# Nine tokens of a head on each partition, and 32x32 turns on VectorE in place of DMA and TensorE ones

## The chip, the cores and the metric

The kernel runs on one core of a Trainium2 chip. The metric is the device time of one execution in microseconds (us); smaller is better. The five engines of the core are TensorE (PE, with its weight loads PEld), VectorE (DVE), ScalarE (ACT), GpSimd (POOL) and SyncE (SP, which here only issues DMAs). Each engine works through its own list of instructions in order.

## The reference, cut to what matters

Eight batches of eight heads, 576 tokens of 64 features, go through a Nystrom attention with 32 landmarks, and its output through a multiplicative feed-forward layer:

```python
q_lm = q.reshape(B, H, 32, 18, 64).mean(axis=3)      # landmarks: means of 18 tokens
k_lm = k.reshape(B, H, 32, 18, 64).mean(axis=3)
A  = softmax(q @ k_lm.T / 8)        # 576 x 32
Bm = softmax(q_lm @ k_lm.T / 8)     # 32 x 32
C  = softmax(q_lm @ k.T / 8)        # 32 x 576
Z  = Bm.T / (norm1(Bm) * norminf(Bm))
for _ in range(6):
    Z = 2 * Z - Z @ Bm @ Z
x = A @ Z @ C @ v                   # 576 x 64 for each head
out = ((x @ w1) * (x @ w2)) @ w3 @ w_out
```

## The kernel before

All work is placed by hand: the order of the instructions on each engine is the order in which the Python code issues them. `attention(st)` is a generator for one batch; it is advanced by `steps(at, n)` between the matmuls of the batch before it, so that its chain of small operations lies beside the large ones.

**Start.** `fold` multiplies w3 with w_out once (192 matmuls of 128x512, in pieces that `steps(fd, n)` lets out). Between these pieces stand the attention of batch 0 and the landmarks of batch 1.

**Main loop.** Each batch b has two stretches. In the *up stretch* `up(st, j, w)` is issued 16 times, for j = 0..7 and w = 0 (x @ w1) and w = 1 (x @ w2); each is four matmuls of 128x288 into a `big` buffer of PSUM, of which there are three. The w = 0 result is copied to `a_sb` by ACT (L443), the w = 1 result is multiplied with `a_sb` into `ab` by DVE (L445). In the *down stretch* `down` is issued 8 times (b even) or 10 times (b odd), each four matmuls of 128x512; every second one ends with an ACT copy to `o_sb` (L466) and its output DMAs on SP. The attention of batch b+1 runs beside both, in fourteen steps:

1. landmarks out of `parts` by two matmuls (L201), copied by ACT to `lm` (L206); `qbd` on POOL (L208)
2. scores of Bm (L217), exponential, normalisation and `bt` on DVE (L224 to L230)
3. first half of the scores of C (L242), exponential to `ect` (L246), partial sums on POOL (`presum`)
4. sums of Bm (L266), second half of the scores of C, the norms (DVE), `bmbd` (POOL)
5. L307 and the start values `sz_`, `tz_` of the inverse, the scores of A (L292), C v (`cv`, L323, and its sums L328)
6. to 11. the six rounds of the inverse: 16 small matmuls (L382), then `tz_` and `sz_` on DVE (L387, L389); the denominators of A ride along
12. product with `bmbd` (L404), `zt`
13. and 14. `zt` times w1 and w2 (L425), read out by ACT (L429) and DVE (L431)

In the up stretch the steps are spread by the tuple `(1, 1, 1, 0, 1, 0, 1, 0)` over j (each after the w = 0 part), one follows the loop, and then comes one step after each `down`.

**What feeds attention.** q and k are loaded by POOL's queue as fp16 `qkn`, with six tokens of a head on each of 96 partitions. SP's queue turns them by DMA into `qkT` (L106), at the head of the up stretch of batch b for batch b+2; for batch 0 TensorE does it (`turn_on_pe`, L117). `landmarks`, on POOL, adds up the tokens of each landmark in six operations for k and six for q (L183 to L192). It is issued at j = 5 of the up stretch, for batch b+2; between its operations POOL issues the four load pieces of q and k of batch b+3 (`qk_pieces`, L93). v comes in four pieces on SP, each behind a small ACT copy (L84).

Of the kernel before, what the change touches and what calls it, by code (L numbers as in the profile page):

```python
# [7 lines left out]
FP32 = mybir.dt.float32  # L8
FP16 = mybir.dt.float16
AXF = mybir.ActivationFunctionType  # L10
# [15 lines left out]
NP = 96  # L26
# [5 lines left out]
def kernel(  # L32
# [34 lines left out]

    def load_qk(st, b):
        qkn = pin.tile([128, 2, H, 384], FP16, name="qkn")
        for t, src in ((1, k), (0, q)):  # L70
            nc.gpsimd.dma_start(out=qkn[0:NP, t, :, :],
                                in_=src[b].rearrange("h (p r) d -> p h (r d)", p=NP))
        st["qkn"] = qkn

    def load_v(st, b):
        vt = st["vt"] if "vt" in st else pin.tile([128, H, 384], FP32, name="vt")
        nc.sync.dma_start(out=vt[0:NP], in_=v[b].rearrange("h (p r) d -> p h (r d)", p=NP))
        st["vt"] = vt

    def load_v_piece(st, b, i, done):  # L80
        if i == 0:
            st["vt"] = pin.tile([128, H, 384], FP32, name="vt")
        hs = slice(2 * i, 2 * i + 2)
        nc.scalar.copy(out=st["vt"][0:NP, 2 * i, 0:1], in_=done)  # L84
        nc.sync.dma_start(out=st["vt"][0:NP, hs],
                          in_=v[b, hs].rearrange("h (p r) d -> p h (r d)", p=NP))

    def qk_pieces(st, b):
        st["qkn"] = pin.tile([128, 2, H, 384], FP16, name="qkn")
        for t, src in ((1, k), (0, q)):  # L90
            for i in range(2):
                hs = slice(4 * i, 4 * i + 4)
                nc.gpsimd.dma_start(out=st["qkn"][0:NP, t, hs, :],  # L93
                                    in_=src[b, hs].rearrange("h (p r) d -> p h (r d)", p=NP))
                yield

# [5 lines left out]
    def transposes(st, t, hs):  # L102
        if "qkT" not in st:
            st["qkT"] = pat.tile([128, 2, H, 3, NP], FP16, name="qkT")
        n = len(hs)
        nc.sync.dma_start_transpose(  # L106
            out=st["qkT"][:, t, hs[0]:hs[0] + n, :, :].rearrange("p h c s -> p (h c) s"),
            in_=st["qkn"][0:NP, t, hs[0]:hs[0] + n, :].rearrange("p h f -> p (h f)"))


    def turn_on_pe(st, t, h0, copy):
        if "qkT" not in st:
            st["qkT"] = pat.tile([128, 2, H, 3, NP], FP16, name="qkT")
        ps = psp.tile([128, 2, 1024], FP16, name="big", bufs=3)
        for i in range(2):
            for n in range(6):
                nc.tensor.transpose(  # L117
                    out=ps[:, i, NP * n:NP * n + NP],
                    in_=st["qkn"][0:NP, t, h0 + 2 * i + n // 3, 128 * (n % 3):128 * (n % 3) + 128],
                    identity=ident16[0:NP, 0:NP])  # L120
        copy(out=st["qkT"][:, t, h0:h0 + 4, :, :].rearrange("p (i h) c s -> p i (h c s)", i=2),
             in_=ps[:, :, 0:6 * NP])
# [3 lines left out]
    ident16 = consts.tile([128, NP], FP16, name="ident16")  # L126
# [3 lines left out]
    nc.gpsimd.tensor_copy(out=ident16, in_=ident[:, 0:NP])  # L130

    def constants():

        mask4 = consts.tile([128, 4, 32], FP32, name="mask4")
        par = consts.tile([128, 2], FP32, name="par")
        ones = consts.tile([128, 1], FP32, name="ones")
        eye = consts.tile([128, 2, 32], FP32, name="eye")
        iit = consts.tile([128, 2, 64], FP16, name="iit")
        onesq = consts.tile([128, 2, 4, 2, 4], FP16, name="onesq")
        nc.vector.memset(mask4, 0.0)  # L140
        nc.vector.memset(par, 0.0)
        nc.vector.memset(ones, 1.0)
        nc.vector.memset(onesq, 0.0)
        for i in range(2):
            sl = slice(64 * i, 64 * i + 64)
            nc.vector.memset(par[sl, i:i + 1], 1.0)
            for jj in range(2):
                nc.vector.tensor_copy(out=iit[sl, jj, :], in_=ident[sl, sl])
# [23 lines left out]
        return mask4, par, ones, eye2, iit, onesq, selc, lomask  # L172


    def landmarks(st, t, eng=nc.gpsimd, pieces=iter(())):
        if "parts" not in st:
            st["parts"] = pz.tile([128, 2, 2, H, 32], FP16, name="parts")
        for h0 in ((0,) if eng is nc.gpsimd else (0, 4)):
            own, n = ("", H) if eng is nc.gpsimd else ("v", 4)
            hs = slice(h0, h0 + n)  # L180
            x = st["qkT"][:, t, hs, :, :]
            tr = pat.tile([128, n, NP], FP32, name="tr" + own, bufs=1)
            eng.tensor_tensor(out=tr, in0=x[:, :, 0, :], in1=x[:, :, 1, :], op=ALU.add)  # L183
            eng.tensor_tensor(out=tr, in0=tr, in1=x[:, :, 2, :], op=ALU.add)  # L184
            next(pieces, None)
            t3 = tr.rearrange("p h (l g) -> p h l g", g=3)
            o = pat.tile([128, n, 32], FP32, name="o3" + own, bufs=1)
            hi, lo = st["parts"][:, 0, t, hs, :], st["parts"][:, 1, t, hs, :]
            eng.tensor_tensor(out=o, in0=t3[:, :, :, 0], in1=t3[:, :, :, 1], op=ALU.add)
            eng.tensor_tensor(out=o, in0=o, in1=t3[:, :, :, 2], op=ALU.add)  # L190
            eng.tensor_copy(out=hi, in_=o)
            eng.tensor_tensor(out=lo, in0=o, in1=hi, op=ALU.subtract)  # L192
            next(pieces, None)


    def attention(st, bank=None):
        bank = bank or small
        qkT, vt, parts = st["qkT"], st["vt"], st["parts"]
        psL = small()
        for i in range(2):  # L200
            nc.tensor.matmul(psL[:, :], iit.rearrange("p a d -> p (a d)"),  # L201
                             parts[:, i].rearrange("p t h l -> p (t h l)"),
                             start=(i == 0), stop=(i == 1))
        pl = psL.rearrange("p (t h l) -> p t h l", t=2, l=32)
        lm = pat.tile([128, 2, H, 32], FP16, name="lm")
        nc.scalar.copy(out=lm, in_=pl)  # L206
        qbd = pat.tile([128, H, 2, 32], FP16, name="qbd")
        nc.gpsimd.tensor_tensor(  # L208
            out=qbd,
            in0=lm[:, 0, :, :].unsqueeze(2).to_broadcast([128, H, 2, 32]),  # L210
            in1=par.unsqueeze(1).unsqueeze(3).to_broadcast([128, H, 2, 32]),
            op=ALU.mult)
        yield
        psB = bank()
        for qd in range(2):
            for h in range(4):
                nc.tensor.matmul(psB[32 * h:32 * h + 32, 32 * qd:32 * qd + 32],  # L217
                                 lm[0:64, 0, 4 * qd + h, :], lm[0:64, 1, 4 * qd + h, :],
                                 start=True, stop=True, tile_position=(0, 32 * h))
# [14 lines left out]
        ects = []  # L234

        def scores_c(qd):
            psC = big()
            pc = psC.rearrange("p a f -> p (a f)")
            for h in range(4):
                for c in range(3):  # L240
                    o = 64 * (3 * h + c)
                    nc.tensor.matmul(pc[0:NP, o:o + 64], qkT[:, 1, 4 * qd + h, c, :],  # L242
                                     qbd[:, 4 * qd + h, :, :].rearrange("p a m -> p (a m)"),
                                     start=True, stop=True)
            ect = pat.tile([128, 4, 6, 32], FP32, name="ect")
            nc.scalar.activation(out=ect[0:NP].rearrange("p h r m -> p (h r m)"),  # L246
                                 in_=pc[0:NP, 0:768], func=AXF.Exp, scale=SCALE / GRP)
            ects.append(ect)

        def presum(qd):  # L250
            e = ects[qd][0:NP]
            t3 = pat.tile([128, 4, 3, 32], FP32, name="t3", bufs=1)
            nc.gpsimd.tensor_tensor(out=t3[0:NP], in0=e[:, :, 0:3, :], in1=e[:, :, 3:6, :],  # L253
                                    op=ALU.add)
            es = pz.tile([128, 4, 32], FP32, name="es")
            nc.gpsimd.tensor_tensor(out=es[0:NP], in0=t3[0:NP, :, 0, :], in1=t3[0:NP, :, 1, :],
                                    op=ALU.add)
            nc.gpsimd.tensor_tensor(out=es[0:NP], in0=es[0:NP], in1=t3[0:NP, :, 2, :], op=ALU.add)
            return es

        scores_c(0)
        es0 = presum(0)
        yield

        psN = small()
        nc.tensor.matmul(psN[:, 0:64], mask4.rearrange("p h m -> p (h m)"),  # L266
                         bm.rearrange("p a m -> p (a m)"), start=True, stop=True)
        scores_c(1)
# [48 lines left out]
        scores_a(0)  # L317
        scores_a(1)

        def cv(qd, es, psV):  # L320
            for r in range(6):
                for h in range(4):
                    nc.tensor.matmul(  # L323
# [358 lines left out]
```

## Time and profile before

| | |
|---|---|
| time, median of 3 runs | 283.07 us (282.11 to 283.45) |
| span of the profiled execution, first to last instruction | 281.0 us |
| PE busy | 269.0 us (96%), 3996 instructions |
| DVE, POOL, ACT busy | 161.8, 161.7, 128.9 us |
| granted TensorE clock, mean | 0.995 |
| DMA packets | 61979, of which 35569 under 512 B |

The profiled execution has no time of its own in the list of runs; its span is 2.1 us under their median, and that much lies around the span. A line of the profile such as `L183 POOL TENSOR_TENSOR tr<-qkT 128x768 f32<-128x768 f16 x16 | 26.3, 1642 | ...` gives the source line, the engine, the operation, output<-input with their sizes, the number of instructions, their busy time in us and the mean duration of one in ns. A line of a timeline gives the start in us, the time from the first start to the last end of a run of equal instructions, the engine, and the rest as above. A matmul's duration includes its way through the array, so the pace of matmuls is read from start to start.

### The profile page before, as it was taken

What the parts mean: (1) busy time and instruction counts of PE and PEld (TensorE: products, weight loads), DVE (VectorE), ACT (ScalarE), POOL (GpSimd) and SP (SyncE); (2) the same over time, 40 slices, a digit from 0 to 9 for tenths busy, and PEclk for the clock granted to TensorE, in tenths of its full rate; (3) what the DMA queues carried; (4) which work ended last, traced back from release to release, by engine and by line L of the source; (5) the groups of instructions that cost most, each with busy time, mean ns of one, the idle gap of its engine ahead of it and who ended that gap; (6) DMA issues with size and microseconds to landing.
All of it is one profiled execution on the core that took longest, in us unless ns stands there. A gap on an engine that the chain in (4) does not pass through costs nothing.

```text
span 281.0 us, 9504 instructions
## 1 busy us (share of the span) xinstructions
PE 269.0 (96%) x3996; PEld 152.0 (54%) x3996; DVE 161.8 (58%) x423; ACT 128.9 (46%) x235; POOL 161.7 (58%) x210
## 2 busy tenths in 40 slices
PE   7999899999999998999999999999999999999993
PEld 3456355444673475447645754574468346734741
DVE  7743134644476675656765765576576755766710
ACT  2643245133662574157427732672276246615531
POOL 1717935396279749944897599459947953500000
PEclk9999999999999999999999999999999999999997
DMA  7999999999717996997699969995999452014024
GB/s 220 322 229 252 203 279 161 161 273 160 128 36 158 224 187 103 160 250 160 134 179 228 159 143 213 227 163 112 222 176 160 124 157 77 5 40 109 6 75 112
DMA packets 61979, 45.57 MB, mean 162 GB/s; under 512 B 35569, under 2 KB 54001, under 8 KB 61937
## 3 DMA queue, kind: packets, MB, share of 16 engines
q1 hardware_dynamic: 47280, 31.93, 48.5%
q0 software_dynamic: 13824, 11.54, 29.8%
q10 hardware_dynamic: 832, 1.51, 1.6%
q8 instruction: 31, 0.51, 0.8%
q14 instruction: 12, 0.09, 0.1%
HBM read 38.80 MB, written 9.44 MB: 172 GB/s over the span
## 4 chain that ended last, share of the span: by engine, by line
PE 84%; POOL 4%; ACT 4%; issue 3%; DVE 1%; DMA 1%; ACTq 0%; DVEq 0%; POOLq 0%
PE big L439 23%; PE acc L457 13%; PE big L457 11%; PE acc L503 10%; PE big L382 6%; PE big L425 5%; ACT a_sb L443 2%; PE small L323 2%; PE big L367 2%; PE acc L323 2%; PE big L490 2%; PE big L242 2%; PE small L503 1%; DMA w3f<-in_moe_w_dram 1%; PE big L292 1%
## 5 line engine op out<-in xcount | busy, mean ns | idle before, releaser
L439 PE MATMUL big<-ahat,gt 128*128 128x288 f16 x512 | 72.2, 286 | 2.0 <-ACT a_sb L443 1.4
L445 DVE TENSOR_TENSOR ab<-a_sb,big 128x576 f16<-128x576 f16 x64 | 48.0, 750 | 27.6 <-PE big L439 15.2
L439 PEld LDWEIGHTS <-gt 128*128 128x128 f16 x512 | 48.4, 98 | 20.3 <-issue 5.6
L443 ACT CAST a_sb<-big 128x576 f16<-128x576 f32 x64 | 40.9, 639 | 32.0 <-PE big L439 31.9
L503 PE MATMUL acc<-wsp,w3t 128*128 128x512 f16 x168 | 40.5, 379 | 0.8 <-ACT w L506 0.5
L457 PE MATMUL acc<-w,ab 128*128 128x512 f16 x160 | 40.3, 381 | 0.0
L457 PEld LDWEIGHTS <-ab 128*128 128x128 f16 x288 | 24.0, 98 | 29.0 <-issue 4.2
L457 PE MATMUL big<-w,ab 128*128 128x512 f16 x128 | 32.7, 381 | 0.0
L466 ACT ACTIVATE o_sb<-acc 128x512 f32<-128x512 f32 (+1 forms) x20 | 11.7, 587 | 42.2 <-PE acc L457 40.6
L183 POOL TENSOR_TENSOR tr<-qkT 128x768 f32<-128x768 f16 x16 | 26.3, 1642 | 7.3 <-DMA qkT<-qkn 7.3
L253 POOL TENSOR_TENSOR t<-ect 96x384 f32<-96x384 f32 x16 | 15.9, 995 | 24.3 <-ACT ect L246 16.3
L503 PEld LDWEIGHTS <-w3t 128*128 128x128 f16 x192 | 18.1, 98 | 20.6 <-issue 1.8
L431 DVE TENSOR_SCALAR gt<-big 128x1024 f16<-128x1024 f32 x16 | 19.6, 1225 | 14.8 <-PE big L425 14.8
L184 POOL TENSOR_TENSOR tr<-tr,qkT 128x768 f32<-128x768 f32 x16 | 26.3, 1642 | 1.3
L208 POOL TENSOR_TENSOR qbd<-lm,par 128x512 f16<-128x512 f16 x8 | 8.3, 1042 | 26.3 <-ACT lm L206 26.3
L429 ACT ACTIVATE gt<-big 128x1024 f16<-128x1024 f32 x16 | 16.4, 1025 | 11.9 <-PE big L425 11.9
L496 DVE SCALAR_TENSOR_TENSOR w3t<-big,w3t 128x512 f16<-128x512 f32 x16 | 11.0, 690 | 17.1 <-ACT w3t L495 17.1
L466 ACT ACTIVATE o_sb<-big 128x512 f32<-128x512 f32 x16 | 9.6, 597 | 18.5 <-PE big L457 18.5
L425 PE MATMUL big<-wup,zt 64*32 64x512 f16 x512 | 17.4, 380 | 0.1
L495 ACT ACTIVATE w3t<-big 128x512 f16<-128x512 f32 x16 | 9.5, 594 | 11.8 <-PE big L490 11.8
L246 ACT ACTIVATE ect<-big 96x768 f32<-96x768 f32 x16 | 12.9, 807 | 3.6 <-PE big L242 2.9
L190 POOL TENSOR_TENSOR o<-o,tr 128x256 f32<-128x256 f32 x16 | 12.9, 807 | 1.3
(317 smaller groups left out, 373.0 us busy)
## 6 DMA issues: line engine op xcount, KB each, us to landing
vt<-in_v_dram SPq DMA_DIRECT2D x28, 288.0 KB, 4.3
out_dram<-o_sb SPq DMA_DIRECT2D x23, 192.0 KB, 3.6
qkn<-in_k_dram POOLq DMA_DIRECT2D x12, 288.0 KB, 5.7
qkn<-in_q_dram POOLq DMA_DIRECT2D x12, 288.0 KB, 6.2
w3f<-in_moe_w_dram SPq DMA_DIRECT2D x6, 512.0 KB, 7.8
out_dram<-o_sb SPq DMA_DIRECT2D x24, 128.0 KB, 3.5
wup<-in_moe_w_dram POOLq DMA_DIRECT2D x4, 512.0 KB, 32.9
out_dram<-o_sb SPq DMA_DIRECT2D x24, 64.0 KB, 3.5
```

Of the source, the lines that this page charges most:

```text
L183: eng.tensor_tensor(out=tr, in0=x[:, :, 0, :], in1=x[:, :, 1, :], op=ALU.add)
L184: eng.tensor_tensor(out=tr, in0=tr, in1=x[:, :, 2, :], op=ALU.add)
L382: nc.tensor.matmul(psI[32 * t:32 * t + 32, qd, o:96], tz_[sl, qd, :], sz_[sl, qd, o:96], start=True, stop=True, tile_position=(32 * h, 32 ...
L425: nc.tensor.matmul(psG[32 * h:32 * h + 32, qd, :], zt[rs, i, h, :], wup[rs, h, w, fs], start=(i == 0), stop=(i == 1), tile_position=(64 * ...
L429: nc.scalar.activation(out=g[:, :, w, fs], in_=psG, func=AXF.Copy, scale=1.0 / ZS)
L431: nc.vector.tensor_scalar(out=g[:, :, w, fs], in0=psG, scalar1=1.0 / ZS, scalar2=None, op0=ALU.mult)
L439: nc.tensor.matmul(p[:, c, 0:HS], st["g"][:, qd, w, 128 * j:128 * j + 128], st["ahat"][qd][:, c, :], start=(qd == 0), stop=(qd == 1))
L443: nc.scalar.copy(out=st["a_sb"], in_=p[:, :, 0:HS])
L445: nc.vector.tensor_tensor(out=st["ab"][:, j, st["t0"]:st["t0"] + S].rearrange("p (c s) -> p c s", c=2), in0=st["a_sb"], in1=p[:, :, 0:HS], ...
L457: nc.tensor.matmul(pso[:, :], ab[:, j, t0:t0 + 128], w34[:, j, :], start=(j == 0), stop=(j == 7))
L466: nc.scalar.activation(out=o_sb[:, c], in_=pso[:, c], func=AXF.Copy, scale=1.0 / (X64 * X64))
L503: nc.tensor.matmul(psW[j][:, :], turned[j, c // 4][:, a, c % 4, :], wsp[:, b, c, :], start=(c == 0 and a + b == 0), stop=(c == 7 and a == 1))
```

## The change

- q, k and v lie with nine tokens of a head on each of 64 partitions, two heads on 128 partitions (`RT = 9`); the output rows follow that order.
- `turn` replaces the DMA transposes and `turn_on_pe`: VectorE transposes 32x32 blocks of 32-bit words, each a pair of neighbouring fp16 features (e = 0, 1). So half the features of a head end on each of two groups of 32 partitions, and a product over the 64 features becomes two accumulating matmuls over 32 rows (e = 0 and e = 1), whose operands are read with a step of two elements.
- A landmark of 18 tokens is two partitions' sums: `landmarks` stays on POOL, with new shapes, and writes `lm` itself; the step-1 matmuls, `parts`, `lm`'s copy and `qbd` go. `exchange`, four copies of 32 partitions on ACT, moves the halves of `lm` between the partition groups.
- The scores of C have the landmarks on the partitions; ACT's exponential also adds up the rows (`accum_out`), which replaces `presum`. VectorE turns the exponentials (`en` to `ent`). C v runs on eight 64x32 tiles of the array, nine rounds.
- The inverse chain carries Bm (32 columns) instead of C v (64 columns); `sz_` is copied by ACT instead of DVE. The product with `xs` comes at the end.
- The places move: `turn_half` is issued after the first four `down` of batch b, for batch b+2; `landmarks` of k follows the second of them and that of q the fourth; v is loaded by four DMAs without ACT copies. The tuple of the up stretch is `(0, 1, 1, 1, 1, 0, 0, 1)`.

```diff
-    def transposes(st, t, hs):
...
-    def turn_on_pe(st, t, h0, copy):
...
+    def turn(st, t, prs):
         if "qkT" not in st:
...
+            st["qkT"] = pat.tile([128, 2, 4, RT, 32, 2], FP16, name="qkT")
+        nc.vector.transpose(
+            out=st["qkT"][:, t, prs].rearrange("p c r q e -> p (c r q e)").bitcast(U32),
+            in_=st["qkn"][:, t, prs, :].rearrange("p c f -> p (c f)").bitcast(U32))
...
+    def landmarks(st, t, pieces=iter(())):
+        if "lm" not in st:
+            st["lm"] = pat.tile([128, 2, 4, 2, 16, 2], FP16, name="lm")
+        x = st["qkT"][:, t].rearrange("p c r q e -> p c r (q e)")
+        add = nc.gpsimd.tensor_tensor
+        tr = pat.tile([128, 4, 4, 64], FP32, name="tr", bufs=1)
+        add(out=tr, in0=x[:, :, 0:4, :], in1=x[:, :, 4:8, :], op=ALU.add)
+        next(pieces, None)
+        add(out=tr[:, :, 0:2, :], in0=tr[:, :, 0:2, :], in1=tr[:, :, 2:4, :], op=ALU.add)
+        add(out=tr[:, :, 0, :], in0=tr[:, :, 0, :], in1=tr[:, :, 1, :], op=ALU.add)
+        add(out=tr[:, :, 0, :], in0=tr[:, :, 0, :], in1=x[:, :, 8, :], op=ALU.add)
+        next(pieces, None)
+        o = tr[:, :, 0, :].rearrange("p c (l g e) -> p c l g e", g=2, e=2)
+        for xh in range(2):
+            add(out=st["lm"][:, t, :, xh], in0=o[:, :, :, 0, :], in1=o[:, :, :, 1, :], op=ALU.add)
+
+    def exchange(st):
+        for a in range(2):
+            for ph in range(2):
+                to, of = 64 * a + 32 * ph, 64 * a + 32 * (1 - ph)
+                nc.scalar.copy(
+                    out=st["lm"][to:to + 32, :, :, 1 - ph].rearrange("p t c l e -> p (t c) (l e)"),
+                    in_=st["lm"][of:of + 32, :, :, 1 - ph].rearrange("p t c l e -> p (t c) (l e)"))
...
+        def scores_c(g):
             psC = big()
...
+            for e in range(2):
+                for c in range(2):
+                    for i in range(4):
+                        to = 32 * (i ^ (2 * (c ^ g)))
+                        sl = slice(32 * i, 32 * i + 32)
+                        nc.tensor.matmul(
+                            psC[to:to + 32, c, 0:HS], lmk(sl, 0, 2 * g + c, e),
+                            qkT[sl, 1, 2 * g + c, :, :, e].rearrange("p r q -> p (r q)"),
+                            start=(e == 0), stop=(e == 1), tile_position=(32 * i, to))
+            for c in range(2):
+                pr = 2 * g + c
+                nc.scalar.activation(out=en[:, pr, :], in_=psC[:, c, 0:HS], func=AXF.Exp,
+                                     scale=SCALE / GRP, accum_out=sums[:, pr:pr + 1])
+            nc.vector.transpose(out=ent[:, 2 * g:2 * g + 2].rearrange("p c r m -> p (c r m)"),
+                                in_=en[:, 2 * g:2 * g + 2, :].rearrange("p c f -> p (c f)"))
...
+        for r in range(RT):
+            for qd, o, pr, sl in tiles:
+                nc.tensor.matmul(psV[qd][32 * o:32 * o + 32, 0:64], ent[sl, pr, r, :],
+                                 vt[sl, pr, 64 * r:64 * r + 64], start=(r == 0), stop=(r == RT - 1),
+                                 tile_position=(sl.start, 32 * o))
...
-                sz_ = pz.tile([128, 2, 96], FP32, name="sz_")
-                nc.vector.tensor_copy(out=sz_, in_=psI[:, :, 0:96])
+                sz_ = pz.tile([128, 2, 64], FP32, name="sz_")
+                nc.scalar.copy(out=sz_, in_=psI[:, :, 0:64])
             else:
-                xd = pz.tile([128, 2, 64], FP32, name="xd")
-                nc.vector.tensor_copy(out=xd, in_=psI[:, :, 32:96])
+                wbd = pz.tile([128, 2, 4, 32], FP32, name="wbd")
+                nc.vector.tensor_tensor(
+                    out=wbd, in0=psI[:, :, 32:64].unsqueeze(2).to_broadcast([128, 2, 4, 32]),
+                    in1=mask4.unsqueeze(1).to_broadcast([128, 2, 4, 32]), op=ALU.mult)
...
-        if b + 2 < B:
-            turn_all(b + 2)
...
-            steps(at, (1, 1, 1, 0, 1, 0, 1, 0)[j])
-            if b + 2 < B and j > 5:
-                load_v_piece(sts[b + 2], b + 2, j - 6, ident[0:NP, 0:1])
+            steps(at, (0, 1, 1, 1, 1, 0, 0, 1)[j])
             up(st, j, 1)
-            if b + 2 < B and j == 5:
-                pieces = qk_pieces(sts[b + 3], b + 3) if b + 3 < B else iter(())
-                landmarks(sts[b + 2], 1, pieces=pieces)
-                landmarks(sts[b + 2], 0, pieces=pieces)
...
             down(ab, b - b % 2, chunks[n // 2], n % 2, hold, bank)
-            if b + 2 < B and n in (1, 3):
-                load_v_piece(sts[b + 2], b + 2, 2 + n // 2, ident[0:NP, 0:1])
             steps(at)
+            if b + 2 < B:
+                if n < 4:
+                    turn_half(b + 2, n)
+                if n == 1:
+                    load_v(sts[b + 2], b + 2)
+                    pieces = qk_pieces(sts[b + 3], b + 3) if b + 3 < B else iter(())
+                    landmarks(sts[b + 2], 1, pieces=pieces)
+                if n == 3:
+                    landmarks(sts[b + 2], 0, pieces=pieces)
```

## The prediction

> **What bounds the kernel now.** I read the page first, then TensorE's timeline for one up stretch, then POOL's and VectorE's timelines for a down stretch, and the duration of the one VectorE transpose that exists.
>
> The page, its busy times and its chain of work:
>
> ```profile
> PE 269.0 (96%) x3996; PEld 152.0 (54%) x3996; DVE 161.8 (58%) x423; ACT 128.9 (46%) x235; POOL 161.7 (58%) x210
> PE 84%; POOL 4%; ACT 4%; issue 3%; DVE 1%; DMA 1%; ACTq 0%; DVEq 0%; POOLq 0%
> ```
>
> TensorE is on the chain for 84%: work taken off it counts, and so does anything that makes it wait. DMAs, 1% of the chain, are hidden; fewer packets are worth nothing by themselves.
>
> TensorE's timeline, up stretch of batch 3:
>
> ```profile
> 152.25 0.59 PE L201 MATMUL small<-parts,iit 128*128 128x512 f16 x2
> ...
> 153.76 0.22 PE L217 MATMUL acc<-lm 64*32 64x32 f16 x8
> 153.91 1.15 PE L439 MATMUL big<-ahat,gt 128*128 128x288 f16 x8
> 154.90 0.69 PE L242 MATMUL big<-qbd,qkT 128*96 128x64 f16 x12
> ...
> 161.00 0.57 PE L292 MATMUL big<-qkT,lm 64*32 64x288 f16 x16
> 161.50 0.88 PE L323 MATMUL small<-vt,ect 96*32 96x64 f32 x48
> ...
> 163.07 1.64 PE L439 MATMUL big<-ahat,gt 128*128 128x288 f16 x12
> 164.65 0.40 PE L382 MATMUL big<-sz__2907,tz__2908 32*32 32x96 f32 x16
> ```
>
> From start to start: two `up` parts take 0.99, so one takes 0.49 (0.12 a matmul). The up stretch lasts from 151.75 to 164.65, 12.9 us (12.87 in batch 0). The attention's small groups fill it without a gap worth naming.
>
> POOL's timeline, landmarks issued in batch 2:
>
> ```profile
> 137.03 1.64 POOL L183 TENSOR_TENSOR tr<-qkT 128x768 f32<-128x768 f16 x1
> 138.75 1.64 POOL L184 TENSOR_TENSOR tr<-tr,qkT 128x768 f32<-128x768 f32 x1
> 140.33 0.72 POOL L93 DMA_DIRECT2D qkn<-in_k_dram  x1
> 141.06 0.64 POOL L189 TENSOR_TENSOR o<-tr 128x256 f32<-128x256 f32 x1
> 141.78 0.81 POOL L190 TENSOR_TENSOR o<-o,tr 128x256 f32<-128x256 f32 x1
> ...
> 150.56 0.68 POOL L192 TENSOR_TENSOR parts<-o,parts 128x256 f16<-128x256 f32 x1
> ```
>
> They run for 14.2 us and end at 151.24; L201 needs them at 152.25. One microsecond is all the slack there is, although they start at 137.03, which is 1.8 us *before* the first inverse group of that batch (L382 at 138.85, as 164.65 is in the next). I call that group's start T0.
>
> VectorE's timeline in the down stretch (its chain for one inverse round, rounds 1.29 apart), and the transpose:
>
> ```profile
> 166.73 0.23 DVE L387 TENSOR_TENSOR tz__3059<-big,eye 128x64 f32<-128x64 f32 x1 [0.27 <-PE big L382]
> 166.87 0.35 DVE L389 COPY sz__3061<-big 128x192 f32<-128x192 f32 x1
> 167.13 0.46 DVE L352 RECIPROCAL small<-small 128x48 f32<-128x48 f32 x1
> ```
> ```profile
> L230 DVE STREAM_TRANSPOSE bt<-bm x8: 245/245/247, 39.0 to 236.5; 128x64 f32<-128x64 f32 x8
> ```
>
> **Matmuls, in an up stretch.** Removed: L201, 152.25 to 152.68, 0.43. Scores of C: now 0.89 (154.90 to 155.79) plus 0.57 in the second group; then two groups of 16 matmuls in two rounds of eight 32x32 tiles, 2 x 0.12, plus about 0.23 for entering and leaving the small tiles (four down matmuls take 0.97 before an L382, where eight in a row take 1.74; L425, four rounds of eight tiles, 0.99 for 0.86 of streaming): 0.96 in all, -0.5. C v: 1.57 now (161.50 to 163.07); 24 matmuls, shown as 48, are six rounds of 0.115, so nine rounds on eight tiles side by side are 1.04, with sums 1.25, -0.32; if the tiles did not overlap, +0.8. Scores of A: two more rounds, +0.24. Bm's scores +0.06. Sum -1.0 us in each of seven batches. No row shows an fp16 operand read with a step of two; L323 streams 4-byte elements at the pace above, so I take no loss; at half pace eight rounds cost 0.12 each, +1.0.
>
> On small tiles there is a rule against the change: the Trainium skill, TensorEngine Tiling (Array Packing), Key Properties, says that a change of tiling mode drains the array. The rows show it at 0.1 us on the way in. Without a drain the scores of C would gain 0.2 us more per batch.
>
> **The landmarks move behind the turns.** This is the term that decides. A turn of half an operand is 576 words: 0.245 for 64, so at one element per 1.04 ns (L445: 576 in 0.75) 0.78 us. VectorE's queue from T0: the last `ab` until 1.0, tz and reciprocal until 1.7; round 1 (result at 1.9) until 2.65; first turn until 3.45; round 2 until 4.2; second turn until 4.95. Only then may POOL add k: at T0 + 5.0 instead of T0 - 1.8.
>
> POOL's new sums per operand: 1024 elements at L183's rate 2.19; 512: 1.14 (qbd, 512 elements, takes 1.04); two of 256: 0.73 each (0.64 to 0.81 in the rows above); two of 128: 0.45 each (presum's 128 take 0.45). That is 5.7, against 5.8 before: the new layout saves POOL nothing here. With two DMA issues of 0.7 and gaps, 7.3 per operand, 14.6 for both; bounds 12.8 (rates of the quickest rows, cheaper issues) and 15.8. What POOL saves (presum, qbd, bmbd) lies elsewhere in time. So `lm` is complete at T0 + 19.6.
>
> Then `exchange`: four ACT copies of 256 elements. A one-element SBUF copy takes 0.18 (L84), 512 elements from SBUF 0.62 (L483): 0.40 each, 1.6 together (bounds 1.0 and 1.8), against 0.59 for L206. The Bm scores can start at T0 + 21.25. TensorE stands before them in order, after five `up` parts and a short wait, 2.7 us into the up stretch. That stretch starts at T0 + 12.9 (b even) or T0 + 14.55 (b odd, two more `down`), so TensorE arrives at T0 + 15.6 or T0 + 17.25 and idles 5.65 or 4.0 us. Behind the waiting copies ACT's `a_sb` queue up, and behind these VectorE's products; behind the waiting scores stand all later `up` parts. Five batches have it: three turned in even b, two in odd. For batch 1 (landmarks in the start) and batch 7 (no DMA issues between its sums, 11.8 us) `lm` is in time, and only the copies count: ready 2.3 + 1.65 into the stretch, 1.25 late. Sum: 3 x 5.65 + 2 x 4.0 + 2 x 1.25 = 27.5 us.
>
> **VectorE's turns of C.** Two of 0.78 join the up stretch, in order between the products. Down the queues from the Bm scores: `a_sb`, exponential 0.9; L224 to L230 1.0; `ab` of j = 2, 2.6; the next `up` part waits for that buffer, then `a_sb` 4.0; two exponentials of C 4.85; turn 5.6; norms 6.3; `ab` of j = 4, 7.05; `a_sb` of j = 6, 7.7; `up` 8.2; L307, scores of A, C v, last `up`, 10.9. TensorE alone has 9.3 us of work there. I take +1.5 (bounds 0 and 2). With -1.0 that is +0.5 in seven batches: +3.5.
>
> **The down stretch.** With 64 columns an L382 group takes 0.27 (the last round now) instead of 0.33: -0.32. The turns make VectorE 1.5 to 1.7 us per round against 1.24 for TensorE; the slack of 0.25 a round is used up by round 4, +0.45. ACT's `sz_` copy, about 0.27 (L409: 128x128 in 0.27), replaces 0.35. Six batches at +0.1, one at -0.3: +0.3. v's loads go earlier on SP, ahead of output stores; nobody waits for either.
>
> **The start.** TensorE's 48 transposes, 2 x 1.02, and L201's 0.97 go. But `lm` of batch 0 still hangs on POOL: sums from 22.9 (its guard copy waits for q), 11.8 long, plus 1.6, 36.4, against 36.3 now. So little is gained before the Bm scores (37.8 now, -1.3) and some behind: -2 (0 to -3).
>
> **Sum.** 281.0 + 27.5 + 3.5 + 0.3 - 2.0 = 310.3 in the profiled execution's own terms; the median stands 2.1 above it: 312 us.
>
> The Trainium skill, TensorE: Matmul & The Clock Gate, Part 1, adds that an idle window of 3.4 us halves the clock. The page's clock row stays at 9 until the end, and no gap in the middle is longer than 1.5 us, so this trace shows no such fall; by the rule some of the five gaps would cost a further 2 us or so each, an estimate from that page.
>
> **The rivals.**
> - *Faster.* The matmuls saved come through. It needs the sums and issues on POOL to end 2.3 us into the up stretch: 10.2 us or less for both operands, where rows say 12.8 to 15.8. Then 281.0 - 7 x 1.0 - 7 x 0.3 - 2 = 270 and, if the copies still delay TensorE 1.25 each, 279; 272 to 281 with the 2.1. For it: TensorE's 84%. Against: POOL's rows. 8%; no change, by chance between, 2%.
> - *Late, but less.* POOL at its lower bound (-1.8 in five batches), copies of 0.25, and VectorE's queue not in the way: 290 to 300. 18%.
> - *Worse.* The first warm-up matmuls (L568) take 0.53 each against 0.38 for the same shape later; if TensorE falls back to that pace in the gaps, or the step of two halves the streaming (+7), 318 to 330. 12%.
> - The forecast, 300 to 318: 60%.
>
> The range 293 to 327 leaves out the first rival and the tails of the others. A measurement of this kernel can tell about 0.5% from no change. Faster 8%, within it 2%, slower 90%.
>
> **What would show it.** Right: in the profile after, TensorE idle before L198 by 4 to 6 us in five batches, ACT's L177 released by POOL's L171, POOL's first L163 of a batch about 5 us after the first L360; C v near 1.25. Wrong: `lm` ready before the second `a_sb` copy of the stretch, POOL's twelve sums within 10 us, or an up stretch under 13 us.

## The result: slower by 19%, and more than forecast

The changed kernel takes 335.77 us (333.32 to 338.10) against 282.59 us for the kernel before on the same chip: the ratio is 1.190, with a 95% interval of 1.183 to 1.198. The forecast was 312 us in a range of 293 to 327. The direction and the main mechanism held; the size did not.

The page of the profile after, its busy times, the granted clock and the chain:

```profile
span 335.2 us, 10503 instructions
PE 284.7 (85%) x4572; PEld 150.4 (45%) x4572; DVE 178.6 (53%) x419; ACT 146.4 (44%) x317; POOL 114.4 (34%) x145
PEclk9999599999999599979996999878996999999999
PE 40%; POOL 21%; DVE 11%; issue 10%; ACT 9%; DMA 6%; SPq 1%; ACTq 0%; DVEq 0%; POOLq 0%
```

TensorE was 96% busy and is 85% busy; it carried 84% of the chain and carries 40%. POOL is now 21% of the chain: the landmarks set the pace. Two entries were not in the forecast's sum: the clock row, which before stood at 9 to the end, has dips, and "issue" (time in which TensorE waited for nothing that the profile shows) has grown from 3% to 10%.

What TensorE waited for, whole span (total, number, longest, in us):

```profile
PE acc L198 <- ACT lm L177: 20.5, 19, 3.9
PE big L419 <- ACT a_sb L423: 5.2, 14, 1.8
PE acc L305 <- issue: 3.2, 3, 2.1
PE acc L479 <- ACT w L482: 2.9, 2, 2.7
PE small L305 <- issue: 2.0, 2, 1.1
PE big L360 <- issue: 1.4, 2, 1.0
```

The first line is the forecast's wait: the scores of Bm (L198) wait for the exchange copies (L177). POOL's timeline behind it, landmarks turned in the down stretch of batch 0, whose first inverse group starts at 90.45:

```profile
95.07 2.13 POOL L163 TENSOR_TENSOR tr<-qkT 128x1024 f32<-128x1024 f16 x1 [10.88 <-DVE qkT L114]
...
102.29 2.12 POOL L163 TENSOR_TENSOR tr<-qkT 128x1024 f32<-128x1024 f16 x1
...
108.63 0.76 POOL L171 TENSOR_TENSOR lm<-tr 128x128 f16<-128x128 f32 x2
```

And ScalarE's, just after:

```profile
109.42 1.66 ACT L177 COPY lm<-lm 32x256 f16<-32x256 f16 x4 [3.76 <-POOL lm L171]
111.11 0.64 ACT L423 CAST a_sb<-big 128x576 f16<-128x576 f32 x1
```

POOL starts 4.6 us after the inverse group (forecast 5.0), is done 18.9 us after it (19.6), and the four copies take 1.66 (1.6). The eviction `a_sb` stands behind them. Now TensorE's timeline over the same place:

```profile
109.88 0.20 PE L198 MATMUL acc<-lm 32*32 32x32 f16 x1 [3.91 <-ACT lm L177]
110.72 0.21 PE L198 MATMUL acc<-lm 32*32 32x32 f16 x2 [0.63 <-ACT lm L177]
111.14 0.28 PE L198 MATMUL acc<-lm 32*32 32x32 f16 x13 [0.22 <-ACT lm L177]
111.36 2.10 PE L419 MATMUL big<-ahat,gt 128*128 128x288 f16 x8
...
114.18 2.08 PE L419 MATMUL big<-ahat,gt 128*128 128x288 f16 x8
```

After the wait, eight `up` matmuls take 2.10 us; in batch 0, where there is no such wait, they take 1.08. The table by windows shows why; in each row stand the window, its length, the busy time of five engines, and then, third from the end, the granted clock:

```profile
106.00:110.00 4.00, 0.12 (x1) 0.10 (x1) 0.45 (x1) 0.55 (x2) 3.21 (x6) 0.98 1.08 214
110.00:112.00 2.00, 1.15 (x19) 0.70 (x19) 0.09 (x1) 1.81 (x5) 0.00 (x0) 0.50 0.79 127
112.00:114.00 2.00, 2.00 (x23) 0.76 (x21) 1.40 (x5) 0.51 (x1) 0.00 (x0) 0.50 0.00 0
114.00:116.00 2.00, 1.88 (x16) 1.29 (x9) 0.82 (x2) 1.13 (x5) 0.00 (x0) 0.50 0.00 0
118.00:120.00 2.00, 1.33 (x10) 0.77 (x8) 1.92 (x6) 0.64 (x1) 0.29 (x1) 1.00 0.00 0
```

The clock is 1.00 before the wait, 0.50 after it until 116.7, and then 1.00 again. And in C v of the same batch, TensorE stops in the middle of a run of short matmuls with no operand missing:

```profile
123.61 0.22 PE L305 MATMUL small<-vt,ent 64*32 64x64 f32 x1
124.67 0.25 PE L305 MATMUL small<-vt,ent 64*32 64x64 f32 x3 [0.85 <-issue]
```

The up stretches of batches 0 to 6 took 16.9, 23.0, 19.3, 21.3, 22.7, 23.4 and 16.4 us, where 12.9 was usual. The down stretches without a gap took 12.5 and 14.2 to 14.3 (before 12.8 and 14.55).

### The profile page after: what moved, and what is told of

Read it like the earlier page. It is cut to its first block, busy times and chain, and to the rows that moved or that the text cites. A ratio compares the mean times of both kernels' runs of the same rounds, so it can differ in the third digit from the quotient of the medians.

```text
span 335.2 us, 10503 instructions
## 1 busy us (share of the span) xinstructions
PE 284.7 (85%) x4572; PEld 150.4 (45%) x4572; DVE 178.6 (53%) x419; ACT 146.4 (44%) x317; POOL 114.4 (34%) x145
## 3 DMA queue, kind: packets, MB, share of 16 engines
q10 hardware_dynamic: 800, 1.44, 1.2%
## 4 chain that ended last, share of the span: by engine, by line
PE 40%; POOL 21%; DVE 11%; issue 10%; ACT 9%; DMA 6%; SPq 1%; ACTq 0%; DVEq 0%; POOLq 0%
PE big L419 12%; PE acc L479 6%; PE acc L437 5%; POOL tr L163 5%; POOL tr L165 5%; ACT a_sb L423 4%; POOL qkn L72 3%; DMA qkn<-in_q_dram 3%; ACT lm L177 3%; PE big L437 3%; POOL lm L171 3%; PE big L360 3%; POOL tr L166 3%; POOL tr L167 2%; PE acc L305 2%
## 5 line engine op out<-in xcount | busy, mean ns | idle before, releaser
L419 PE MATMUL big<-ahat,gt 128*128 128x288 f16 x512 | 83.3, 308 | 9.8 <-ACT a_sb L423 5.2
L419 PEld LDWEIGHTS <-gt 128*128 128x128 f16 x512 | 51.3, 103 | 38.0 <-issue 22.4
L163 POOL TENSOR_TENSOR tr<-qkT 128x1024 f32<-128x1024 f16 x16 | 34.0, 2126 | 74.0 <-DVE qkT L114 73.3
L411 DVE TENSOR_SCALAR gt<-big 128x1024 f16<-128x1024 f32 x16 | 19.6, 1224 | 14.3 <-PE big L405 14.3
L114 DVE STREAM_TRANSPOSE qkT<-qkn 128x576 uint32<-128x576 uint32 (+1 forms) x30 | 23.9, 797 | 0.0
L235 DVE STREAM_TRANSPOSE ent<-en 128x576 f32<-128x576 f32 x16 | 12.5, 778 | 20.9 <-ACT en L233 20.9
L198 PE MATMUL acc<-lm 32*32 32x32 f16 x112 | 4.6, 185 | 20.5 <-ACT lm L177 20.5
L409 ACT ACTIVATE gt<-big 128x1024 f16<-128x1024 f32 x16 | 16.4, 1023 | 11.9 <-PE big L405 11.9
L165 POOL TENSOR_TENSOR tr<-tr 128x512 f32<-128x512 f32 x16 | 20.4, 1275 | 0.6
L177 ACT COPY lm<-lm 32x256 f16<-32x256 f16 x32 | 12.8, 401 | 17.1 <-POOL lm L171 16.6
L305 PE MATMUL small<-vt,ent 64*32 64x64 f32 x576 | 15.0, 225 | 2.0 <-issue 2.0
L305 PE MATMUL acc<-vt,ent 64*32 64x64 f32 x504 | 11.9, 224 | 5.2 <-issue 3.2
```

Of the source, the lines that this page charges most:

```text
L114: nc.vector.transpose(out=st["qkT"][:, t, prs].rearrange("p c r q e -> p (c r q e)").bitcast(U32), in_=st["qkn"][:, t, prs, :].rearrange(" ...
L163: add(out=tr, in0=x[:, :, 0:4, :], in1=x[:, :, 4:8, :], op=ALU.add)
L165: add(out=tr[:, :, 0:2, :], in0=tr[:, :, 0:2, :], in1=tr[:, :, 2:4, :], op=ALU.add)
L177: nc.scalar.copy(out=st["lm"][to:to + 32, :, :, 1 - ph].rearrange("p t c l e -> p (t c) (l e)"), in_=st["lm"][of:of + 32, :, :, 1 - ph].re ...
L305: nc.tensor.matmul(psV[qd][32 * o:32 * o + 32, 0:64], ent[sl, pr, r, :], vt[sl, pr, 64 * r:64 * r + 64], start=(r == 0), stop=(r == RT - 1 ...
L411: nc.vector.tensor_scalar(out=g[:, :, w, fs], in0=psG, scalar1=1.0 / ZS, scalar2=None, op0=ALU.mult)
```

## Experiments

Eleven of the twelve runs were timed against the kernel before; the ratio is of those, and a difference between two ratios is turned into us with 282.6.

| run | what is changed | ratio (95%) |
|---|---|---|
| after | the change | 1.190 (1.183 to 1.198) |
| e1_fill | idle time filled with repeated `up` matmuls | 1.159 (1.147 to 1.171) |
| e3_split | C v in two parts with two `up` parts between | 1.155 (1.144 to 1.166) |
| e2_early | k's turns and sums in the up stretch | 1.101 (1.090 to 1.111) |
| e4_early_ahead | e2, exchange ahead of the up stretch on ScalarE | 1.117 (1.107 to 1.127) |
| e7_early_poolx | e2, exchange on GpSimd behind the sums | 1.069 (1.061 to 1.076) |
| e6_early_half_instr | e2, C v with half the instructions | 1.058 (1.048 to 1.067) |
| e9_comb | e2 + e7 + e6 | 1.031 (1.024 to 1.038) |
| e10_comb_v | e9, loads of v behind the last store | 1.019 (1.011 to 1.027) |
| e11_comb_v_noturn | e10 without the turns of C | 0.988 (0.984 to 0.992) |
| e8_before_inverse | the kernel before with the new inverse alone | 0.992 (0.989 to 0.995) |
| e12_before_best | e8 with half the instructions in C v | 0.968 (0.963 to 0.973) |

**Late landmarks, and the clock behind them.** Two runs separate the wait from what follows it.

```diff
-            up(st, j, 0)
+            up(st, j, 0, (0, 7, 3, 7, 3, 7, 0, 0)[b] if j == 2 else 0)   # so many repeats
```

> The idle 2.4 to 4.1 us before the scores of Bm are filled with repeats of the up part just before them (7 more groups of four matmuls, 3.4 us, in batches 1, 3 and 5; 3 more, 1.5 us, in 2 and 4); the same numbers are written again, nothing else changes and TensorE has more work. If the five falls of the clock after those gaps are a cost of their own, the granted clock stays at 1.0 there, eight up matmuls after the scores take 1.0 us again instead of 2.0, and the time falls by about 8.5 us (6 to 11) although the landmarks are as late as before. If the gaps cost only their own length, and the up stretch after them is long because of the order on VectorE and ScalarE, the time stays within 2 us or rises.

It fell by 9 us by the ratios (6.8 by the medians), with 27 groups of extra work and the landmarks as late as before. In batch 1 the clock stayed up:

```profile
108.30:110.00 1.70, 0.41 (x4) 0.18 (x3) 0.00 (x0) 1.57 (x4) 0.04 (x1) 1.00 1.11 156
110.00:112.00 2.00, 1.73 (x37) 1.09 (x38) 1.04 (x5) 1.33 (x4) 0.00 (x0) 1.00 0.39 65
```

So the slow clock was a cost of its own. It did not vanish altogether: in batch 3 the clock still fell, after gaps of 0.50, 0.65 and 0.35 us, the same as those of batch 1, where it did not. Of the 8.5 us between the two profiled executions, 1.3 lie in the start, which the repeats do not touch; the 7.1 in the main loop are the part that it can claim.

```diff
+        # in attention, behind the first tz_, ahead of scores_a
+        for f in st.pop("late", ()): f()       # turn k of b + 2 twice, landmarks of k
...
-                if n < 4:
-                    turn_half(b + 2, n)
+                if n < 2:
+                    turn_half(b + 2, n + 2)    # q; its landmarks at n == 1
```

> The two turns of k and the sums of k move from the down stretch to the end of the up stretch before it (behind the first tz of the inverse, where VectorE has nothing to do for 2.9 us during C v); the turns of q go into the first two rounds of the inverse. The landmarks should then be complete about 12.5 us after the first inverse group instead of 19, before TensorE comes to the Bm scores. If the lateness and the clock that falls with it carry the loss, 17 us of idle time and about 8.5 us of slow clock go: 310 us (305 to 315). If the turns in the up stretch hold up what VectorE owes TensorE there, less than 15 us come back: above 320.

It came to 312.1 us, within what the first theory expected: 25 us of the 54 go with lateness and the clock that falls with it. The turns found their place during C v at no visible price.

**The exchange.**

```diff
-            steps(at, (0, 1, 1, 1, 1, 0, 0, 1)[j])
+            steps(at, (0, 0, 1, 1, 1, 0, 0, 1)[j])
...
         steps(at, 30)
+        steps(nxt, 1)                       # exchange, ahead of the up stretch
         at = nxt
```

> As with the early turns and sums, and ScalarE's four exchange copies stand ahead of the up stretch instead of between its second and third part. If the copies cost TensorE 1.25 us in each of seven batches because they stand between two evictions, this is 6 to 9 us faster than the early turns alone: about 302 us. If they only take the place of another wait, it is within 2 us of it.

The expectation was wrong: 4 to 5 us slower than e2, not 6 to 9 faster. In five of seven batches the copies only took the place of another wait: there the up stretches of the two runs differ by 0.3 us at most. TensorE, batch 3 of that run:

```profile
163.82 2.06 PE L421 MATMUL big<-ahat,gt 128*128 128x288 f16 x12
166.92 1.44 PE L421 MATMUL big<-ahat,gt 128*128 128x288 f16 x8 [1.03 <-ACT a_sb L425]
168.29 0.27 PE L198 MATMUL acc<-lm 32*32 32x32 f16 x16
```

The scores of Bm no longer wait, but the fourth `up` part does, for the first eviction, which now stands behind the copies. In batches 2 and 4 this gap is 2.2 and 3.1 us, and the up stretch 2.1 and 3.1 us longer than in e2. POOL had `lm` complete 3.0 and 4.6 us before the copies there; what the copies stood behind on ScalarE was an eviction to `o_sb` that had waited 1.9 and 2.8 us itself. After both gaps the clock was 0.50, for 3.41 and 6.83 us.

```diff
-                nc.scalar.copy(out=st["lm"][...], in_=st["lm"][...])       # in attention
+                nc.gpsimd.tensor_copy(out=st["lm"][...], in_=st["lm"][...])  # behind landmarks(q)
```

> On the kernel with the early turns and sums, the four exchange copies stand on GpSimd right behind the sums of q instead of on ScalarE in the up stretch. Four copies of about 0.4 us end 14.2 us after the first inverse group, before TensorE comes to the scores of Bm. If the copies delay the evictions of the up stretch, the 1.25 us in each of seven batches come back, and the 2.7 us stall of the start, where an eviction of the fold stands behind copies that wait for the landmarks, goes too: 299 to 304 us. If the up stretch is held by VectorE's order, it stays at 309 to 312.

9 us less than e2. On GpSimd the copies hold nobody in the main loop. The 16 matmuls of the Bm scores (L198, here L197) take 0.20 us from their first start to the next `up`, against 1.44 to 1.48 in the changed kernel:

```profile
102.36 0.27 PE L197 MATMUL acc<-lm 32*32 32x32 f16 x16
102.56 1.15 PE L420 MATMUL big<-ahat,gt 128*128 128x288 f16 x8
```

The 2.65 us stall of the fold in the start is gone too. So the exchange was dear for its place in ScalarE's queue, not for its 1.66 us.

**C v: its size and its gaps.** In batch 2 of the changed kernel 144 matmuls (72, each counted twice) take 1.89 us from first to last. One wait of 0.46 lies between two starts, for the bank that the first tz_ is read from (the profile calls 0.25 of it idle):

```profile
156.84 0.32 PE L305 MATMUL small<-vt,ent 64*32 64x64 f32 x8
157.40 0.26 PE L305 MATMUL acc<-vt,ent 64*32 64x64 f32 x4 [0.25 <-DVE tz__2400 L288]
```

The rest is 10.0 ns each on average. The forecast had 1.04 for all. Two runs ask what holds them.

```diff
-    psV[...][..., 0:64], ent[sl, pr, r, :], vt[sl, pr, 64 * r:64 * r + 64]
+    psV[...][..., 0:n],  ent[sl, pr, r, :], vt[sl, pr, 64 * r:64 * r + n]   # n = 64 if r == 0 else 32
```

> The changed kernel with C v on 32 of the 64 columns of v in eight of its nine blocks of tokens (the rest of the product is left out, so the output is not the reference's); the number of its instructions stays. C v without a gap took 1.89 us in batches 2 and 3 (144 matmuls as the profile counts them, 12.9 ns each). If its eight tiles are held up by the number of instructions, it stays at 1.8 to 1.9 us. If they are held up by the columns that they stream, it falls to about 1.05 us.

Run once, 333.1 us: in batch 2, 1.77 us for 144, 9.2 ns each without the wait. Half the columns bought 0.12 us, so columns do not set it.

```diff
-    ent[sl, pr, r, :],        vt[sl, pr, 64 * r:64 * r + 64]
+    upper(ent[sl, pr, r, :]), upper(vt[sl, pr, 64 * r:64 * r + 64])   # bfloat16 view, every second element
```

> On the kernel with the early turns and sums, the fp32 operands of C v are read as the upper 16 bits of each element, as bfloat16: the lower bits are left out, each matmul is one instruction in the profile instead of two, and 72 stand where 144 stood. If the gaps in and behind C v (8.7 us in the early kernel's seven batches) come from a program that arrives too slowly for so many short instructions, C v falls to about 0.95 us and the gaps go with it: 296 to 300 us. If the gaps have another cause, only C v's own 0.93 in seven batches comes back: about 305.5.

It took 12 us off e2 by the ratios. C v is 0.99 us in six batches: 72 matmuls, the same wait of 0.46, and 7.5 ns each without it. Of the gaps above 0.3 us in C v of the seven batches only one of 0.5 in batch 6 is left; one of 0.4 stands in the denominators of batch 1, and one of 1.4 in the start. Batch 3:

```profile
172.55 0.21 PE L311 MATMUL small<-vt,ent 64*32 64x64 bf16 x4
173.03 0.21 PE L311 MATMUL acc<-vt,ent 64*32 64x64 bf16 x4 [0.26 <-DVE tz__2993 L288]
...
173.52 0.22 PE L311 MATMUL acc<-vt,ent 64*32 64x64 bf16 x4
```

The average hides two paces: the matmuls of the first half, right behind the wait, start about 4 ns apart, and after a pause of 0.10 us those of the second half 8.3. In the second half of C v the changed kernel has 10.0 and the run with half the columns 8.7. So a run of such matmuls costs 8.3 to 10 ns for each one issued, whether it streams 64 columns or 32, fp32 or bfloat16; whether the matmul or the weight load that goes with each sets this pace, no run tells. On the four tiles of the kernel before it was another limit: four fp32 matmuls start 7 ns apart and the next four follow after another 36, which makes 56 ns a round, or 14.5 ns for each matmul with the pauses. Eight tiles instead of four took off a third, not a half, and there are 144 matmuls instead of 96.

```diff
         for r in range(RT):
+            if r == 4 and bank is acc:
+                yield                       # two up parts come here
...
-            steps(at, (0, 1, 1, 1, 1, 0, 0, 1)[j])
+            steps(at, (0, 1, 1, 1, 1, 0, 1, 1)[j])
```

> C v is cut after four of its nine blocks of tokens, and the scores of A with the first part go one step earlier, so that two up parts (1 us, 16 instructions) lie between the two parts of C v. If the gaps of 0.5 to 2.1 us inside or just behind C v come from TensorE's program arriving too slowly for 320 instructions in 2.1 us, most of them go, and with them the half clock after the longest: 4 to 7 us less. If they come from a wait that the trace does not name, or from a fixed place in the program, they move along and the time stays within 2 us.

10 us less than the changed kernel by the ratios (8.5 by the medians), somewhat more than the first theory's 4 to 7. The gaps in batches 0 to 5 at L305 and L360 of 0.91, 0.85, 0.33, 1.03, 2.12, 1.10 us (6.3 together) became 0.95, 0.65 and 0.71 (2.3), and the half clock behind the longest went too. The clock was 0.50 for 30.7 us in the profiled execution, against 41.0; part of that lies behind the landmarks and in the start, which the split does not aim at, and the remaining gain is not traced further.

Where the gaps come from shows in the trace's DMA records. The queue that carries instructions moved 36 blocks of 16,384 bytes (packets, MB, share of the DMA engines):

```profile
q8 instruction: 36, 0.59, 0.7%
```

TensorE ran 9,144 instructions, 254 for each block; e6, with 1,152 fewer, has 31 blocks. In batches 0 to 5 each gap ends 1.34 to 1.37 us after the arrival of a block: in batch 1 it arrived at 123.31 and the matmuls resume at 124.67, in batch 4 at 229.96 and 231.31. C v and its sums are 320 instructions in 2.1 us, and a block takes 0.9 to 1.6 us to move. The one long gap in the kernel before (1.3 us at L328 in batch 1) has nearly the same mark: block at 108.20, matmul at 109.67. In the start, the gap of 0.8 us in C v ends 1.7 us after a block.

**The three repairs together.**

> The three repairs together on the changed kernel: k's turns and sums in the up stretch, the exchange on GpSimd, C v from the upper 16 bits of its fp32 operands (half the instructions; the lower bits are left out). If lateness with its slow clock, the exchange and C v's instructions are separate costs, the last one takes 11 us off the 302 as it did from the 312: 291 us (288 to 294). If they share their time, less than 6 us go: above 296.

291.3 us, as expected: the three costs add up. The code is that of the three runs above.

**The loads of v.**

```diff
                 if n == 1:
-                    load_v(sts[b + 2], b + 2)
                     landmarks(sts[b + 2], 0, pieces=pieces)
...
+                if n == nd - 1:
+                    load_v(sts[b + 2], b + 2)
```

> As the three repairs, and the four loads of v are issued behind the last output store of a down stretch instead of behind its first part. If the two waits of ScalarE for an o_sb buffer whose store stands behind v on SP (2.6 and 2.1 us in the run before) reach TensorE, 1 to 3 us less than without; if they are covered, within 1 us.

Some 3.4 us less by the ratios (4.6 by the medians), with intervals that still overlap by 0.3%. The rows that tell it apart, ScalarE's waits in e9 and then in e10:

```profile
ACT o_sb L451 <- DMA out_dram<-o_sb: 5.4, 2, 3.6
```
```profile
ACT o_sb L451 <- DMA out_dram<-o_sb: 3.5, 2, 1.8
```

In e9 TensorE idled 2.1 us in batch 4 behind the longer wait; in e10 no batch has such a gap. The gap is no accident of one execution: it stands in batch 4 of e2, e6 and e7 as well (1.1, 2.3 and 1.1 us), and is missing again in e11. In the changed kernel itself the wait was 3.3 us (one), and lay under the wait for the landmarks.

**VectorE's turns of C.**

```diff
-            nc.vector.transpose(out=ent[...], in_=en[...])
+            # left out; ent is a view of en
```

> As the run before, without VectorE's two turns of the exponentials of C: C v reads them unturned, so its product is not that of the reference, and their buffer is double. If the two turns of 0.78 us delay the products that TensorE waits for in the middle of the up stretch, as the forecast put it (1.5 us a batch), about 7 to 10 us less; if they hide, within 2 us.

8.6 us less. The up stretches are 12.4 and 13.0 us where e10 has 13.6 and 14.2: 1.2 us a batch, from two turns of 0.78. This is the price of the new layout that no reordering here removed. Without it the kernel is 1.2% below the kernel before, but with C v at the upper 16 bits, which helps the kernel before as well: e12 below, with the same C v, is at 0.968.

**The part that pays, alone.**

```diff
-    psI[..., o:96], tz_[sl, qd, :], sz_[sl, qd, o:96]     # sz_ = R and x; copy on VectorE
+    psI[..., o:64], tz_[sl, qd, :], sz_[sl, qd, o:64]     # sz_ = R and Bm; copy on ScalarE, x in xs
```

> The kernel of before with one part of the change alone: the inverse chain carries Bm (64 columns instead of 96), ScalarE copies sz_, and x stays outside the chain. The forecast's step: an inverse group takes 0.27 instead of 0.33 us, five times a batch, so 0.3 us less in each of seven batches: 2.1 us, ratio 0.993. If ScalarE's copy comes later than VectorE's did, because of the output evictions in its queue, the gain is given back: 1.00 or above.

Ratio 0.992, as forecast for this part: down stretches of 12.4 and 14.2 us against 12.8 and 14.55.

> The kernel of before with the inverse chain on Bm and its own C v (four tiles of 96x32) read from the upper 16 bits of each fp32 operand, the lower bits left out: 48 instructions where 96 stood. If TensorE's time per instruction sets C v there too, its 1.39 us fall to 0.7 in each of seven batches and the one supply gap of 1.3 us in it goes: 274 us, 5 to 6 less than the inverse alone (280.1). If TensorE then only waits for the evictions around it, less than 2 us come back: 278 or more.

272.5 us, ratio 0.968, faster than either kernel: every up stretch is 12.2 us (12.9 before), and the supply gap is gone. It carries C v at the precision of the upper 16 bits only, which the kernel before does not. At that precision, the new layout with all its repairs (e10, 1.019) is 5% slower than the old one. On e12's four tiles a bfloat16 matmul took 7.7 ns (without one wait of 0.30 us), about as much as on eight (7.5 in e6). TensorE is 96% busy in it:

```profile
span 269.0 us, 8681 instructions
PE 258.6 (96%) x3612; PEld 144.4 (54%) x3612; DVE 152.0 (56%) x383; ACT 139.0 (52%) x275; POOL 155.6 (58%) x202
```

## Why the prediction was right in kind and wrong in size

**Right: the late landmarks.** The forecast's largest term was 27.5 us. Measured: 17.2 us of idle time before the first L198 of batches 1 to 5 (4.1, 2.4, 4.1, 2.4, 4.1), and 1.27 us more than 0.2 in each of seven L198 groups, 8.9: 26.1 together. In batch 2, 1.8 of the 2.4 stood behind ScalarE's wait for an `o_sb` buffer, but POOL ended `lm` only at 144.95, so the scores could not have begun sooner. Turns, POOL's sums and the copies each came within 0.7 us.

**Wrong: the clock was read and left out of the sum.** The step was "no gap in the middle is longer than 1.5 us, so this trace shows no such fall". That was said of the trace before, but the same sum had just put five gaps of 4.0 to 5.65 us into the kernel. The sentence behind it even had a price, "a further 2 us or so each", close to the 1.2 to 2.0 us measured, and left it out of the 310.3. After each of these five the clock was 0.50 for 3.41 or 6.83 us; each group of eight `up` matmuls behind the scores took 0.5 to 0.95 us longer than in batch 0, with L227 and L242 8.3 us over five batches, and e1 gave back about 7. The Trainium skill, TensorE: Matmul & The Clock Gate, Part 1, was right that the clock halves; it names an idle window of 3.4 us, but here the clock also fell in batches 2 and 4, where no single gap before it was longer than 2.4 us, and in batch 3 of e1, where none was longer than 0.65.

**Wrong: TensorE's instructions were taken as free.** C v was "nine rounds on eight tiles side by side ... 1.04, with sums 1.25"; it is 1.89 and 0.25, so this term is 0.9 us short in each of seven batches, 6.2 in all (0.46 of each is a wait for a PSUM bank). The round time of 0.115 us was carried over from four tiles as if tiles set it; on eight, the 8.3 to 10 ns for each matmul set it. The gaps of supply were not in the sum at all, although the forecast had the only one of the kernel before in view; they are 6.3 us, and 1.6 more of slow clock behind the longest, less the 1.3 that the span before held already: 6.6.

**Wrong: the start.** Forecast -2.0, measured +2.2 (first `up` matmul at 73.6, before at 71.3). The fold's eviction L482 stands behind copies that wait for the landmarks: TensorE waits 2.65 us, and its clock is 0.50 from 34.8 to 41.6. But the first `up` matmul lay between 70.9 and 75.4 in the profiled executions of the changed kernel and its variants, so this size is uncertain.

**Smaller terms.** VectorE's turns of C were put at 1.5 us a batch; e11 shows 1.2, so 2.1 us too much in seven. The down stretch was put at +0.3 in all; apart from the gaps and the slow clock counted above it came to -1.7, 2.0 us too much. The loads of v: "nobody waits for either" was wrong, by 3.4 us once the landmarks no longer covered it.

By these, 310.3 + 8.3 + 6.2 + 6.6 + 4.2 - 1.4 - 2.1 - 2.0 = 330.1, and the profiled execution took 335.2. The remaining 5 us, some 0.7 in each up stretch, are not assigned. Waits for `a_sb` evictions behind the exponentials of C lie there (0.35 and 0.22 us in batch 0, behind the two groups of scores), and each of the four exponentials of a batch is now followed by a read of its sum, 0.20 us on ScalarE, which the forecast did not have; no run took these away.

The rival named "worse" had the right mechanism in the slow clock, but its 318 to 330 has nothing of C v's matmuls, the supply of instructions or the start. Its other condition did not come: the rounds of the scores of C, read with a step of two, follow each other after 0.14 us, and those of A after 0.13, where half pace would take 0.24.

## What to carry to other kernels

When a sum puts a new wait on TensorE, price what the wait does to the matmuls behind it: here a wait of 2.4 to 4.1 us cost another 1.2 to 2.0 us of slow clock in the same batch. Count instructions as well as columns: here eight tiles instead of four brought fp32 matmuls from 14.5 to 10.0 ns apart, not to 7, and a run of 320 instructions in 2.1 us outpaced its own program. Before moving a step, ask what stands behind it in its new queue: the same four copies cost 9 us less on an engine where no eviction was queued behind them.

## What the runs showed of the hardware

- On eight 64x32 tiles, in the second half of C v, a matmul started every 10.0 ns (64 columns, fp32), 8.7 (32 columns, fp32) or 8.3 (64 columns, bfloat16). On four 96x32 tiles, over all of C v, it was every 14.5 ns in fp32 and, without one wait, every 7.7 in bfloat16 (e12).
- TensorE's program came in blocks of 16,384 bytes, some 254 instructions; in batches 0 to 5 of the changed kernel six gaps of 0.3 to 2.1 us all ended 1.34 to 1.37 us after a block had landed.
- The granted clock changed in steps of 3.41 us. It fell to 0.50 after a wait of 1.8 us (batch 2, with two shorter ones behind it), in e1 even after three of 0.50, 0.65 and 0.35 us, and came back 3.41 or 6.83 us later. The same three gaps in another batch of e1, and one of 2.3 us in a third, brought no fall. What share of a stretch must be busy was not settled.
